# Output products that stream the gated tile, with block transposes as evacuation and one distance between streamed and loaded tiles

## The chip, the cores and the metric

One core of a Trainium2 chip runs the kernel. The metric is the device time of one execution in microseconds, the median of several runs. Shorter is better.

## What is computed

The reference is a gated linear recurrence per head, followed by a feed-forward block:

```python
# q, k, v, a: 4 batches, 8 heads, 768 positions, 48 wide
scale = np.minimum(mag, 0.999) / (mag + 1e-06)     # mag = |a_re + i a_im|
for t in range(S):
    new_re = ar * S_re - ai * S_im
    new_im = ar * S_im + ai * S_re
    kv = np.einsum('bhd,bhe->bhde', k[:, :, t], v[:, :, t])
    S_re, S_im = new_re + kv, new_im
    y[:, :, t] = np.einsum('bhd,bhde->bhe', q[:, :, t], S_re)
...
# x: 3072 tokens x 384; w_gate, w_val: 384 x 1536; w_out: 1536 x 384
g = x @ w_gate
silu = g * (1.0 / (1.0 + np.exp(-g)))
return (silu * (x @ w_val)) @ w_out
```

## The kernel before

**Tiling.** The 3072 tokens are 24 slabs of 128: six chunks of the sequence for each of four batches. Two slabs of one chunk make a group; there are 12 groups, 0 to 11, and groups 10 and 11 hold the last chunk. For each group `stage_ops` loads a, q and k and turns them into scaled queries and keys (ScalarE and VectorE, with cumulative sums over positions on TensorE, lines 500 and 503). For each slab `slab_ops` makes scores (L691, tiles p_ps, "strips" of 64 columns of the array), new states (L757, L760), and then products with the states and with the values (L691 into p_py, strips of 32 columns, four column groups side by side). ScalarE and VectorE copy p_py out as a high part xh and a rest xl (L780, L787), because the matmuls take a reduced 32-bit type (float32r).

**Feed-forward.** `ffn_ops` goes over 12 blocks f of 128 hidden units for each group of 256 tokens. One block is called a step here. f1 (L942) computes gate and value for 128 hidden units x 256 tokens: the weights are the loaded (stationary) tile, xh or xl streams past it, 256 columns; with high and low parts three products for each of three slices of the model width, for gate and value: 18 matmuls. ScalarE applies silu (L948), VectorE multiplies by the value (L953, tile sg), and sg is split again into hh and hl (L354 or L356, L350). f2 (L976) is the output product: hh or hl of 128 tokens is loaded, and 384 columns of the output weights stream; three products for each of two halves of the tokens: 6 matmuls into p_po. In group 0 there are no parts: one product of plain 32-bit floats each. f2 of a block comes one or two f1 later in TensorE's order.

After a group's last f2, `ev` copies each half of p_po to ost, on ScalarE (L354) or on VectorE (L356), and `st` stores ost with one DMA (L990) from SP's queue. p_po is a pair of tiles, one for each half, each with its own bank; the next group's first f2 waits until they are copied out.

**Output weights.** They arrive as doubles in 32-bit words. `c1` to `c3` make plain floats; `c4` casts the high part (lines 354 and 356), `c5` subtracts for the low part (L350). The high and low parts of a block lie behind each other in one tile of 2 x 384 columns.

**Order.** A planner in the program (class `Planner`) fixes the order of all engines' work from costs and due times; each operation is then written out in that order, and each engine works its own list in order. The change leaves the planner's costs and rules alone, so operations stand in the same order after it as before; what an operation issues is different.

**Addresses.** The tiles xh, xl, hh and hl have 128 spare columns; GATED (for hh and hl) and INPUT (for xh and xl) say how many of these come ahead of the data. STILL, with two filler tiles, shifts the weights of f1. These numbers set how far a streamed tile starts from the tile that is loaded. Modulo 512 bytes, worked out from the addresses of the built program, that distance is 192 in every f1, 448 in every f2 of groups 1 to 11, and 128 in the cumulative sums of L503.

```python
TURN_OVER, STILL, GATED, INPUT = 128, 96, 16, 16
...
slots = dict(qs=1, ks=1, T=2, dec=3, sc=2, sg=2, hh=2, hl=2, ost=2, xh=2, xl=2, vt=2, vr=2,
             gv=2, po=1, ps=2, py=1, pm=1)
...
pl.add("oe" + I, {"ACT": 0.4, "DVE": 0.5} if g < NGRP - 1 else {("ACT", "DVE")[i]: 0.45}, ev, deps=[f"f2_{g}.{NF - 1}"], alloc=[("ost", I)], use=[("po", g)], key=key)
```

Of the kernel before, what the change touches and what calls it, by code (L numbers as in the profile page):

```python
# [9 lines left out]
F32 = mybir.dt.float32  # L10
# [4 lines left out]
ALU = mybir.AluOpType  # L15
# [4 lines left out]
P = 128  # L20
# [36 lines left out]

TURN_OVER, STILL, GATED, INPUT = 128, 96, 16, 16
HIGH, LOW, WHOLE = 0, 1, 2
# [171 lines left out]
def quick(ctx, tc, q, k, v, a_re, a_im, w_gate, w_val, w_out, out, count):  # L231
# [3 lines left out]
    const = ctx.enter_context(tc.tile_pool(name="const", bufs=1))  # L235
    still = ctx.enter_context(tc.tile_pool(name="still", bufs=1))
    gap = ctx.enter_context(tc.tile_pool(name="gap", bufs=1))
    work = ctx.enter_context(tc.tile_pool(name="work", bufs=1))
# [20 lines left out]
    turned_v = [const.tile([P, 2, 2, 64], F32, name=f"vr{i}") for i in range(2)]  # L259
    still.tile([P, STILL], F32, name="ahead")  # L260
    gap.tile([P, TURN_OVER - STILL], F32, name="behind")
    W, HALVES = {}, {}
    WIDE = {"w": 2 * DM, "o": DM}

    def place(nm, f, dtype):

        pool = still if nm == "w" else work
        return pool.tile([P, 2 * WIDE[nm]], dtype, name=f"w{nm}{f}", tag=f"w{nm}{f}", bufs=1)
# [52 lines left out]
    def new(tag, inst):  # L321
        if tag in fixed:
            t = fixed[tag][0]
        elif tag[0] in ("ww", "wo"):
            t = None
        elif tag in PSUMS:
            t = psum.tile([P, 512], F32, name="p_" + tag, tag=tag, bufs=2 if tag == "po" else slots[tag])
        else:
            shape, dt = SHAPE[tag]
            if isinstance(inst, tuple) and inst[0] in SPLIT:  # L330
                dt = F32R
            if tag == "xh" and inst == 0:
                dt = F32
            if tag == "xl" and isinstance(inst, str):
                dt = U32
            if tag in ("xh", "xl", "hh", "hl"):
                n = math.prod(shape[1:])
                ahead = GATED if tag in ("hh", "hl") else INPUT
                t = work.tile([P, n + TURN_OVER], dt, name=tag, tag=tag, bufs=slots[tag])[:, ahead:ahead + n]
                if len(shape) > 2:  # L340
                    t = t.rearrange("p (k n) -> p k n", k=shape[1])
            else:
                t = work.tile(shape, dt, name=tag, tag=tag, bufs=slots[tag])
                if tag == "dec":
                    t = t[:, 0:4 * H]
        at_[tag, inst] = t
        return t
# [254 lines left out]
    def slab_ops(n):  # L602
# [80 lines left out]

        def strips(turns, width=32):
# [47 lines left out]
        def states(e):  # L732
# [3 lines left out]
            for slot, kt_, pr, o, heads in blocks():  # L736
                turns[slot] += [(o, gf[:, P * pr + col:P * pr + col + 32], qT(h), kt_ == 0 and i == 0, False)
                                for i, (h, col) in enumerate(heads)]
            strips(turns)

        def values(e):
# [8 lines left out]
            strips(turns)  # L750

# [64 lines left out]
    def weight_ops(f):  # L816
        for nm, n, user in (("w", 2 * DM, "f1"), ("o", DM, "f2")):
# [37 lines left out]
            def c4(e, nm=nm, n=n, whole=whole):  # L855
                W.pop((nm, f - 1, WHOLE), None)
                W[nm, f] = place(nm, f - 1, F32R)
                cast(e, W[nm, f][:, 0:n], whole())

            def c5(e, nm=nm, n=n, whole=whole):  # L860
                tt(e, W[nm, f][:, n:2 * n], whole(), W[nm, f][:, 0:n].bitcast(F32), ALU.subtract)

# [64 lines left out]
    def ffn_ops(g):  # L927
        t0, step = (T1 + (g - 1) * NF * FT, FT) if g else (T0, FT0)
        for f in range(NF):
            I = f"{g}.{f}"  # L930
# [35 lines left out]
            def f2(e, f=f, I=I):  # L966
                hh, hl, h = (at_.get((x, I)) for x in ("hh", "hl", "sg"))
                products = ((hh, HIGH), (hh, LOW), (hl, HIGH)) if g else ((h, WHOLE),)
                if f == 0:
                    new("po", f"{g}.0")  # L970
                    new("po", f"{g}.1")
                for i in range(2):
                    cs = slice(i * P, (i + 1) * P)
                    po = at_["po", f"{g}.{i}"][:, :DM]
                    for j, (l, part) in enumerate(products):
                        nc.tensor.matmul(out=po, lhsT=l[:, cs], rhs=weight("o", f, part),  # L976
                                         start=f == 0 and j == 0, stop=f == NF - 1 and j == len(products) - 1)
            PO = [("po", g)]
# [3 lines left out]
        for i in range(2):  # L982
            b, c = where(2 * g + i)
            I = f"{g}.{i}"

            def ev(e, I=I):
                cast(e, new("ost", I), at_["po", I][:, :DM])

            def st(e, I=I, b=b, c=c):
                nc.sync.dma_start(out=out[b * S + c * P:b * S + (c + 1) * P, :], in_=at_["ost", I])  # L990
            key = t0 + NF * step + 4
# [245 lines left out]
```

## Time and profile before

| | |
|---|---|
| time, median of 3 runs | 629.52 us (629.48 to 631.21) |
| the profiled execution | 629.75 us, of which its span is 628.0 us |
| TensorE matmuls busy | 600.1 us, 96% |
| VectorE busy | 502.0 us, 80% |
| ScalarE busy | 405.2 us, 65% |
| GpSimd busy | 4.2 us, 1% |
| granted clock of TensorE, mean over the span | 0.999 |

PE is TensorE's matmul side, PEld its loading of stationary tiles, DVE VectorE, ACT ScalarE, SPq the queue from which SP issues DMAs. A line such as L942 is a line of the kernel before. In a timeline, matmuls of one form that follow each other share a row (x2); the time behind the start is how long they overlapped in flight, so the pace of TensorE is read from start to start.

### The profile page before, as it was taken

The numbers are of one execution on the slowest core, as the hardware profiler recorded it, in microseconds if no ns is written. First come the engines' busy times: TensorE is split into PE (matmuls) and PEld (weight loads), VectorE is DVE, ScalarE is ACT, GpSimd is POOL, SyncE is SP. The second block draws the span as 40 slices with busy tenths as digits, with TensorE's granted clock in tenths as the row PEclk, the third lists the DMA queues.
The fourth block names the chain that finished last, engine by engine and source line by source line (L and its number), as shares of the span: only waits on it lengthen the run. The fifth ranks groups of instructions, "written<-read, shape, count | busy, mean of one in ns | idle before, by whom it ended". The sixth has DMA issues, their size and how long they took to land.

```text
span 628.0 us, 16113 instructions
## 1 busy us (share of the span) xinstructions
PE 600.1 (96%) x6562; PEld 566.9 (90%) x6562; DVE 502.0 (80%) x931; ACT 405.2 (65%) x653; POOL 4.2 (1%) x15
## 2 busy tenths in 40 slices
PE   2699999989999999999999999999999999999996
PEld 1488788978999899999999999999999999999995
DVE  8999999998997878977989869769879768544432
ACT  7865448886796794857876966976966873212210
POOL 2000000000000000000000000000000000000000
PEclk9999999999999999999999999999999999999999
DMA  8899501233635564455366453554464542331100
GB/s 258 230 301 310 204 27 32 64 124 85 161 106 147 132 149 123 129 139 139 91 148 148 108 153 95 144 156 95 136 166 113 146 121 70 101 103 51 52 1 30
DMA packets 155574, 79.89 MB, mean 127 GB/s; under 512 B 116187, under 2 KB 151261, under 8 KB 155494
## 3 DMA queue, kind: packets, MB, share of 16 engines
q1 hardware_dynamic: 155494, 78.80, 46.1%
q8 instruction: 53, 0.87, 0.6%
q14 instruction: 27, 0.22, 0.1%
HBM read 59.83 MB, written 4.78 MB: 103 GB/s over the span
## 4 chain that ended last, share of the span: by engine, by line
PE 83%; DVE 12%; DMA 1%; issue 1%; ACT 1%; SPq 1%; DVEq 0%
PE p_gv L942 42%; PE p_po L976 21%; PE p_py L691 6%; PE p_ps L691 6%; PE p_pm L503 2%; DVE ww L350 2%; PE p_pm L760 2%; PE p_gv L629 2%; DVE sg L953 1%; DVE s L350 1%; PE p_pm L757 1%; DMA wo<-in_q_dram 1%; DVE ks L350 1%; PE p_gv L500 1%; DVE wo L350 1%
## 5 line engine op out<-in xcount | busy, mean ns | idle before, releaser
L942 PE MATMUL p_gv<-xh,ww 128*128 128x256 f32 x1596 | 303.1, 287 | 2.0 <-DVE sg L953 1.3
L942 PEld LDWEIGHTS p_gv<-xh,ww 128*128 128x128 f32 x1596 | 256.0, 189 | 9.1 <-DVE sg L953 2.7
L942 PE MATMUL p_gv<-xl,ww 128*128 128x256 f32 x726 | 201.2, 277 | 0.0
L1068 ACT ACT_TABLE_LOAD x118 | 151.4, 1283 | 2.1
L942 PEld LDWEIGHTS p_gv<-xl,ww 128*128 128x128 f32 x726 | 136.3, 188 | 0.1
L948 ACT ACTIVATE sg<-p_gv 128x256 f32<-128x256 f32 x144 | 54.9, 384 | 123.7 <-PE p_gv L942 122.3
L976 PE MATMUL p_po<-wo,hh 128*128 128x384 f32 x484 | 125.1, 339 | 0.0
L953 DVE TENSOR_TENSOR sg<-sg,p_gv 128x256 f32<-128x256 f32 x144 | 59.0, 412 | 54.9 <-ACT sg L948 54.6
L976 PEld LDWEIGHTS p_po<-wo,hh 128*128 128x128 f32 x484 | 81.2, 188 | 1.6 <-issue 1.6
L976 PE MATMUL p_po<-wo,hl 128*128 128x384 f32 x242 | 80.7, 334 | 0.0
L350 DVE TENSOR_TENSOR hl<-sg,hh 128x256 fp32r<-128x256 f32 x132 | 54.9, 416 | 7.0 <-ACT hh L354 1.8
L976 PEld LDWEIGHTS p_po<-wo,hl 128*128 128x128 f32 x242 | 45.4, 188 | 0.0
L407 ACT ACTIVATE s<-s 128x768 f32<-128x768 f32 x44 | 36.7, 843 | 9.1 <-DVE s L350 6.7
L691 PEld LDWEIGHTS p_ps<-T 96*64 96x64 f32 x768 | 35.9, 138 | 5.0 <-issue 2.4
L691 PE MATMUL p_ps<-T 96*64 96x128 f32 (+1 forms) x768 | 39.4, 254 | 0.0
L719 DVE TENSOR_TENSOR sc<-p_ps,turn 128x512 f32<-128x512 f32 x48 | 32.1, 685 | 5.0 <-PE p_ps L691 4.8
L780 ACT CAST xh<-p_py 128x384 fp32r<-128x384 f32 x22 | 10.5, 480 | 37.6 <-PE p_py L691 37.5
L356 DVE CAST hh<-sg 128x256 fp32r<-128x256 f32 x87 | 25.2, 290 | 6.1 <-PE p_po L976 2.5
L354 ACT CAST hh<-sg 128x256 fp32r<-128x256 f32 x45 | 18.1, 404 | 18.3 <-DVE sg L953 14.4
L691 PE MATMUL p_py<-sc,vr 128*32 128x128 f32 x384 | 26.0, 273 | 0.9 <-issue 0.9
L691 PE MATMUL p_py<-sc,vt 128*32 128x128 f32 x384 | 25.2, 273 | 0.0
L942 PE MATMUL p_gv<-xh,ww-1_292 128*128 128x256 f32 x132 | 24.8, 280 | 0.0
(142 smaller groups left out, 853.9 us busy)
## 6 DMA issues: line engine op xcount, KB each, us to landing
T<-ww SPq DMA_DIRECT2D x216, 64.0 KB, 2.1
wo<-in_moe_w_out_dram SPq DMA_DIRECT2D x24, 384.0 KB, 4.4
ww<-in_moe_w_gate_dram SPq DMA_DIRECT2D x12, 384.0 KB, 5.8
ww<-in_moe_w_val_dram SPq DMA_DIRECT2D x12, 384.0 KB, 6.6
vt<-in_v_dram SPq DMA_DIRECT2D x24, 192.0 KB, 4.0
out_dram<-ost SPq DMA_DIRECT2D x24, 192.0 KB, 2.3
wo<-in_moe_w_gate_dram SPq DMA_DIRECT2D x12, 384.0 KB, 5.4
wo<-in_moe_w_val_dram SPq DMA_DIRECT2D x12, 384.0 KB, 3.6
```

The lines of the kernel that those rows point to most:

```text
L350: V[e].tensor_tensor(out=out, in0=a, in1=b, op=op)
L354: nc.scalar.copy(out=out, in_=in_)
L356: nc.vector.tensor_copy(out=out, in_=in_)
L407: nc.scalar.activation(out=of(to or dst), in_=of(source), func=func, scale=scale, **kw)
L503: nc.tensor.matmul(out=ps, lhsT=tri, rhs=flat(half(x, i)), start=j == 0, stop=j == 1)
L691: nc.tensor.matmul(out=o, lhsT=l, rhs=r, start=opens, stop=closes, tile_position=(0, width * slot), skip_group_check=True)
L719: nc.vector.tensor_tensor(out=s.rearrange("p (r m) t -> p r m t", m=2), in0=scores[qd].rearrange("p (r m) t -> p r m t", m=2), in1=m, op=A ...
L942: nc.tensor.matmul(out=gv[:, i, :], lhsT=l, rhs=r, start=(m == 0), stop=(m == len(mm) - 1))
L948: nc.scalar.activation(out=new("sg", I), in_=at_["gv", I][:, 0:2 * P], func=AF.Silu)
L953: nc.vector.tensor_tensor(out=sg, in0=sg, in1=at_["gv", I][:, 2 * P:4 * P], op=ALU.mult)
L976: nc.tensor.matmul(out=po, lhsT=l[:, cs], rhs=weight("o", f, part), start=f == 0 and j == 0, stop=f == NF - 1 and j == len(products) - 1)
L1068: nc.scalar.preload_act_table_set(op.load)
```

## The change

- f2 of groups 1 to 10 (`upright` is false): the output weights are loaded, 128 output columns at a time, and hh or hl streams, 256 tokens. For each of three pieces k there are three products: nine matmuls (L982 of the changed kernel) that give the transposed result, output columns by tokens, in one tile p_po of two banks. Groups 0 and 11 keep the six matmuls.
- The output weights' columns are stored in another order (`rows_of`, in `c4` and `c5`), in pieces of 32, so that transposing blocks of 32 x 32 gives rows of the output.
- `ev` of the ten groups is a transpose of 32 x 32 blocks out of p_po, always on VectorE (L998); in the last group it undoes the order of the columns.
- `st` of the ten groups is four DMAs of 32 partitions (L1007), each of pieces of 96 columns.
- GATED and INPUT are 48, and the filler tiles are gone: the distance modulo 512 is 192 in f1 and in the new f2, 320 in f2 of group 11, and 128 still in the cumulative sums.
- In the last chunk, the strips of the products with states and values begin with the fourth column group (`first`).

```diff
-TURN_OVER, STILL, GATED, INPUT = 128, 96, 16, 16
+TURN_OVER, GATED, INPUT = 128, 48, 48
...
-    still.tile([P, STILL], F32, name="ahead")
-    gap.tile([P, TURN_OVER - STILL], F32, name="behind")
...
+    def rows_of(nm, at, plain=False):
+
+        if nm != "o":
+            return at
+        return at.rearrange("p (q k m) -> p q k m", k=KT, q=4) if plain else at.rearrange("p (k q m) -> p q k m", k=KT, q=4)
...
-            t = psum.tile([P, 512], F32, name="p_" + tag, tag=tag, bufs=2 if tag == "po" else slots[tag])
+            t = psum.tile([P, 1024 if tag == "po" else 512], F32, name="p_" + tag, tag=tag, bufs=slots[tag])
...
-                slot = min((s for s in range(len(turns)) if turns[s]), key=lambda s: ends[s])
+                slot = min((s for s in range(len(turns)) if turns[s]), key=lambda s: (ends[s], (s + first) % len(turns)))
...
-            strips(turns)
+            strips(turns, first=1 if c == NCH - 1 else 0)
...
-                cast(e, W[nm, f][:, 0:n], whole())
+                cast(e, rows_of(nm, W[nm, f][:, 0:n]), rows_of(nm, whole(), True))
...
+        upright = g in (0, NGRP - 1)
...
+                wh, wl = (weight("o", f, x).rearrange("p (k n) -> p k n", k=KT) for x in (HIGH, LOW))
+                for k in range(KT):
+                    for j, (l, r) in enumerate(((wh, hh), (wl, hh), (wh, hl))):
+                        nc.tensor.matmul(out=po[:, 2 * P * k:2 * P * k + 2 * P], lhsT=l[:, k, :], rhs=r,
+                                         start=f == 0 and j == 0 and k != 1, stop=f == NF - 1 and j == 2, skip_group_check=True)
...
-                cast(e, new("ost", I), at_["po", I][:, :DM])
+                po, o = at_["po", g], new("ost", I)
...
+                    nc.vector.transpose(out=o.rearrange("p (j k m) -> p k j m", j=4, k=KT),
+                                        in_=po[:, 0:2 * P * KT].rearrange("p (k i j m) -> p k i j m", k=KT, i=2, j=4)[:, :, i])
...
+                for q in range(4):
+                    nc.sync.dma_start(out=r.rearrange("(j a) (q n) -> q a j n", a=32, q=4)[q],
+                                      in_=o[32 * q:32 * q + 32].rearrange("a (j n) -> a j n", j=4))
```

**TensorE, the first f2 of group 1** (p_po is its result; of the two tiles behind the arrow the first streams and the second is loaded; behind them the shape of the result), before:

```order
L503 MATMUL p_pm<-re,tri 128x384
L976 MATMUL p_po<-wo-1_344,hh 128x384 x2
L976 MATMUL p_po<-wo-1_344,hl 128x384
L976 MATMUL p_po<-wo-1_344,hh 128x384 x2
L976 MATMUL p_po<-wo-1_344,hl 128x384
L942 MATMUL p_gv<-xh,ww_880 128x256
L942 MATMUL p_gv<-xl,ww_880 128x256
```

and with the change:

```order
L503 MATMUL p_pm<-re,tri 128x384
L982 MATMUL p_po<-hh,wo-1_336 128x256 x2
L982 MATMUL p_po<-hl,wo-1_336 128x256
L982 MATMUL p_po<-hh,wo-1_336 128x256 x2
L982 MATMUL p_po<-hl,wo-1_336 128x256
L982 MATMUL p_po<-hh,wo-1_336 128x256 x2
L982 MATMUL p_po<-hl,wo-1_336 128x256
L943 MATMUL p_gv<-xh,ww_871 128x256
L943 MATMUL p_gv<-xl,ww_871 128x256
```

The gated tile and the weights have changed places, six matmuls of 384 columns have become nine of 256, and what stands around them is as before.

**VectorE at the end of group 1** (flags are sums that are checked at the end of the program, ks and qs the turned keys and queries of a later group), before:

```order
L350 TENSOR_TENSOR ww_1390<-wo_1387,ww_1390 128x768
L446 TENSOR_REDUCE flags<-re 128x1
L923 TENSOR_REDUCE flags<-ww_1390 128x1
L953 TENSOR_TENSOR sg<-sg,p_gv 128x256
L350 TENSOR_TENSOR ks<-kt,s_1761 128x16x48
```

and with the change:

```order
L350 TENSOR_TENSOR ww_1404<-wo_1401,ww_1404 128x768
L446 TENSOR_REDUCE flags<-re 128x1
L923 TENSOR_REDUCE flags<-ww_1404 128x1
L998 STREAM_TRANSPOSE ost<-p_po 128x3x4x32 x2
L954 TENSOR_TENSOR sg<-sg,p_gv 128x256
L350 TENSOR_TENSOR ks<-kt,s_1784 128x16x48
```

Both evacuations of group 1 come from ScalarE's list into VectorE's, ahead of the product that makes a gated tile. Of the other groups' evacuations four more come over from ScalarE (one each in groups 2, 8, 9 and 10); the rest were on VectorE already.

**SP's queue around the store of a half of group 3** (T is a slab's transposed queries and keys, sent in pieces), before:

```order
L658 DMA T<-ww_1390 32x8x64 x3
L680 DMA vr_89<-in_v_dram 64x2x48 x4
L990 DMA out_dram<-ost 128x384
L658 DMA T<-ww_1390 32x8x64 x9
L990 DMA out_dram<-ost 128x384
```

and with the change:

```order
L658 DMA T<-ww_1404 32x8x64 x3
L680 DMA vr_83<-in_v_dram 64x2x48 x4
L1007 DMA out_dram<-ost 32x4x96 x4
L658 DMA T<-ww_1404 32x8x64 x9
L1007 DMA out_dram<-ost 32x4x96 x4
```

Where one store stood between the pieces of T, four stand now.

## Rows read from the trace of the kernel before

**Rows 1.** page: engines' busy time; the chain that ended last, by engine and line.

```profile
PE 600.1 (96%) x6562; PEld 566.9 (90%) x6562; DVE 502.0 (80%) x931; ACT 405.2 (65%) x653; POOL 4.2 (1%) x15
...
PE 83%; DVE 12%; DMA 1%; issue 1%; ACT 1%; SPq 1%; DVEq 0%
PE p_gv L942 42%; PE p_po L976 21%; PE p_py L691 6%; PE p_ps L691 6%; PE p_pm L503 2%; DVE ww L350 2%; PE p_pm L760 2%; PE p_gv L629 2%; DVE sg L953 1%; DVE s L350 1%; PE p_pm L757 1%; DMA wo<-in_q_dram 1%; DVE ks L350 1%; PE p_gv L500 1%; DVE wo L350 1%
```

**Rows 2.** waits of TensorE: us in total, times, longest.

```profile
PE p_gv L500 <- DMA wo<-in_q_dram: 10.5, 1, 10.5
...
PE p_gv L942 <- DVE sg L953: 1.3, 2, 0.9
```

**Rows 3.** windows: length, then busy us of PE, PEld, DVE, ACT, POOL; clock, DMA.

```profile
100.00:150.00 50.00, 47.09 (x476) 43.65 (x475) 47.66 (x87) 42.22 (x65) 0.00 (x0) 1.00 0.28 79
300.00:400.00 100.00, 100.00 (x1211) 98.03 (x1209) 86.43 (x158) 76.37 (x115) 0.00 (x0) 1.00 0.50 127
```

**Rows 4.** windows: four steps, all lines; one f2, L976 alone.

```profile
347.97:360.38 12.41, 12.41 (x97) 12.38 (x97) 10.29 (x20) 12.23 (x17) 0.00 (x0) 1.00 0.36 87
...
303.68:304.73 1.05, 1.05 (x6) 0.90 (x6) 1.00 0.25 92
```

**Rows 5.** windows, L942 alone (PE, PEld): one f1 behind a cumulative sum, one elsewhere.

```profile
243.43:245.47 2.04, 2.04 (x18) 2.00 (x18) 1.00 1.04 368
232.04:234.16 2.12, 2.12 (x18) 2.08 (x18) 1.00 0.27 76
```

**Rows 6.** windows, L942 alone: five f1 behind value strips; one f1 after the second.

```profile
298.42:300.58 2.16, 2.16 (x18) 2.13 (x18) 1.00 0.00 0
341.57:343.80 2.23, 2.23 (x18) 2.18 (x18) 1.00 0.49 164
386.90:389.07 2.17, 2.17 (x18) 2.13 (x18) 1.00 0.00 0
434.24:436.46 2.22, 2.22 (x18) 2.17 (x18) 1.00 0.00 0
480.89:483.11 2.22, 2.22 (x18) 2.15 (x18) 1.00 0.23 24
...
344.87:346.92 2.05, 2.05 (x18) 2.02 (x18) 1.00 0.77 241
```

**Rows 7.** lines with shapes apart: count | busy us, mean ns of one | idle before.

```profile
L350 DVE TENSOR_TENSOR ks<-kt,s 128x768 f32<-128x768 f32 x22 | 20.9, 950 | 2.3 <-ACT s L407 2.2 <-PE p_pm L760 0.2
...
L649 DVE STREAM_TRANSPOSE ww<-ks 128x768 f32<-128x768 f32 x18 | 17.5, 973 | 1.7 <-DMA T<-ww 1.6
...
L356 DVE COPY ost<-p_po 128x384 f32<-128x384 f32 x16 | 8.6, 548 | 1.7 <-PE p_po L976 1.7
...
L356 DVE CAST wo<-wo 128x384 fp32r<-128x384 f32 x7 | 2.5, 352 | 0.0
```

**Rows 8.** timeline of VectorE and TensorE at the end of group 5.

```profile
357.86 1.01 DVE L356 COPY ost<-p_po 128x384 f32<-128x384 f32 x2
...
359.34 0.34 PE L976 MATMUL p_po<-wo-1_344,hh 128*128 128x384 f32 x1
```

**Rows 9.** end of group 1: window, timeline of ScalarE and of TensorE.

```profile
161.07:172.70 11.63, 11.63 (x90) 11.35 (x88) 11.63 (x18) 10.17 (x18) 0.00 (x0) 1.00 0.57 162
...
163.90 0.85 ACT L354 COPY ost<-p_po 128x384 f32<-128x384 f32 x2
...
173.19 0.39 PE L942 MATMUL p_gv<-xh,ww 128*128 128x256 f32 x1 [0.45 <-DVE sg L953]
```

**Rows 10.** timeline of SP's queue and TensorE near 264 us; page: issues to landing.

```profile
263.51 0.54 SPq L990 DMA_DIRECT2D out_dram<-ost  x1
264.10 5.87 SPq L658 DMA_DIRECT2D T<-ww  x9
...
275.08 0.58 PE L691 MATMUL p_ps<-T 96*64 96x128 f32 x8
...
T<-ww SPq DMA_DIRECT2D x216, 64.0 KB, 2.1
```

More of the change, by code (lines that the diff above doesn't have):

```diff
@@ L265, in place @@
     def place(nm, f, dtype):
-        pool = still if nm == "w" else work
-        return pool.tile([P, 2 * WIDE[nm]], dtype, name=f"w{nm}{f}", tag=f"w{nm}{f}", bufs=1)
+        return work.tile([P, 2 * WIDE[nm]], dtype, name=f"w{nm}{f}", tag=f"w{nm}{f}", bufs=1)
     def spare(nm):
@@ L682, in slab_ops, with strips @@
         pl.add("ldr" + N, {"SP": 2.20}, ldr, deps=[f"ldr{n - 1}"] if n else [], alloc=[("vr", n)], lat=1.4, move=0.8, wary=WARY)
-        def strips(turns, width=32):
+        def strips(turns, width=32, first=0):
             ends = [0] * len(turns)
             while any(turns):
-                slot = min((s for s in range(len(turns)) if turns[s]), key=lambda s: ends[s])
+                slot = min((s for s in range(len(turns)) if turns[s]), key=lambda s: (ends[s], (s + first) % len(turns)))
                 o, l, r, opens, closes = turns[slot].pop(0)
@@ L749, in values @@
                                         c == 0 and kt_ == 0 and i == 0, i == len(heads) - 1))
-            strips(turns)
+            strips(turns, first=1 if c == NCH - 1 else 0)
         def kv(e):
@@ L857, in c4 @@
                 W[nm, f] = place(nm, f - 1, F32R)
-                cast(e, W[nm, f][:, 0:n], whole())
+                cast(e, rows_of(nm, W[nm, f][:, 0:n]), rows_of(nm, whole(), True))
             def c5(e, nm=nm, n=n, whole=whole):
-                tt(e, W[nm, f][:, n:2 * n], whole(), W[nm, f][:, 0:n].bitcast(F32), ALU.subtract)
+                tt(e, rows_of(nm, W[nm, f][:, n:2 * n]), rows_of(nm, whole(), True), rows_of(nm, W[nm, f][:, 0:n].bitcast(F32)), ALU.subtract)
             pl.add("c1" + N, cost(("DVE2",), n), c1, deps=loads + ([f"c3{f - 1}{nm}"] if f else []),
@@ L967, in f2 @@
                 hh, hl, h = (at_.get((x, I)) for x in ("hh", "hl", "sg"))
-                products = ((hh, HIGH), (hh, LOW), (hl, HIGH)) if g else ((h, WHOLE),)
                 if f == 0:
[L970 to L977, printed above, removed]
+                    new("po", g)
+                po = at_["po", g]
+                if upright:
+                    products = ((hh, HIGH), (hh, LOW), (hl, HIGH)) if g else ((h, WHOLE),)
+                    for i in range(2):
+                        for j, (l, part) in enumerate(products):
+                            nc.tensor.matmul(out=po[:, 512 * i:512 * i + DM], lhsT=l[:, P * i:P * i + P], rhs=weight("o", f, part),
+                                             start=f == 0 and j == 0, stop=f == NF - 1 and j == len(products) - 1)
+                    return
+                wh, wl = (weight("o", f, x).rearrange("p (k n) -> p k n", k=KT) for x in (HIGH, LOW))
[3 more added lines that the diff above has]
+                                         start=f == 0 and j == 0 and k != 1, stop=f == NF - 1 and j == 2, skip_group_check=True)
             PO = [("po", g)]
@@ L984, in ffn_ops, with ev @@
             I = f"{g}.{i}"
-            def ev(e, I=I):
-                cast(e, new("ost", I), at_["po", I][:, :DM])
-            def st(e, I=I, b=b, c=c):
-                nc.sync.dma_start(out=out[b * S + c * P:b * S + (c + 1) * P, :], in_=at_["ost", I])
+            def ev(e, i=i, I=I):
+                po, o = at_["po", g], new("ost", I)
+                if upright:
+                    part = po[:, 512 * i:512 * i + DM]
+                    cast(e, *((rows_of("o", x, plain) for x, plain in ((o, True), (part, False))) if g else (o, part)))
+                else:
+                    nc.vector.transpose(out=o.rearrange("p (j k m) -> p k j m", j=4, k=KT),
+                                        in_=po[:, 0:2 * P * KT].rearrange("p (k i j m) -> p k i j m", k=KT, i=2, j=4)[:, :, i])
+            def st(e, I=I, b=b, c=c):
+                r, o = out[b * S + c * P:b * S + (c + 1) * P, :], at_["ost", I]
+                if upright:
+                    nc.sync.dma_start(out=r, in_=o)
+                    return
+                for q in range(4):
+                    nc.sync.dma_start(out=r.rearrange("(j a) (q n) -> q a j n", a=32, q=4)[q],
+                                      in_=o[32 * q:32 * q + 32].rearrange("a (j n) -> a j n", j=4))
             key = t0 + NF * step + 4
```

2 lines of the change are left out of this document (removed).

## The prediction

> **What bounds the kernel now.** I read the page first: TensorE is busy for 600.1 of 628.0 us and carries 83% of the chain that ended last, the gate and value products (L942, from here f1) 42% and the output products (L976, f2) 21% [rows 1]. The view of waits says where TensorE is not the bound: its long wait is the first load, and later only short waits on VectorE are left [rows 2]. By stage, from 300 to 400 us TensorE is busy throughout and VectorE for 86 of 100 us; from 100 to 150 us VectorE is the fuller one, 47.66 to 47.09 of 50 [rows 3]. So from group 2 on the time is the sum of TensorE's steps, and I price the change by the start times of its matmuls. Their busy time is no price: it contains overlap.
>
> A step is one f1 (18 matmuls of 256 columns) and one f2 (6 of 384). Four steps in a row take 12.41 us, 3.1025 each (96 matmuls; one more touches the edge); one f2 takes 1.05 us [rows 4] and one f1 2.05 [rows 6]. That is 0.114 us for 256 columns and 0.175 for 384: the wide form costs more per column, not less.
>
> The second thing to see is that f1 has two beats. Behind cumulative sums 18 matmuls take 2.04 us, 0.1133 each; at other places the same 18, same shapes, take 2.12 us, 0.1178 each [rows 5]. Both keep their beat through the whole f1. Of the five f1 that directly follow value strips (those of the second slab, groups 5 to 9), two are on the short beat (2.16 and 2.17 us, the first gap included) and three on the long one (2.22 to 2.23) [rows 6]. After the first of the long ones, one f2 suffices and the next f1 is back at 2.05 [rows 6].
>
> **The change, part by part.**
>
> 1. Output products. Nine matmuls of 256 columns replace six of 384: as many columns (2304). They now have f1's shape, and, by the constants, f1's distance between the streamed and the loaded tile. So I give them f1's price. On the short beat a step becomes 27 x 0.1133 = 3.06 us. Against 3.1025 that is a gain of 0.0425. Groups 2 to 10 have 108 such steps in the stretch where TensorE is the bound: 108 x 0.0425 = 4.6 us gained. Group 1's twelve would give 0.5 more, but lie where VectorE is as full as TensorE; I count them as nothing and keep 0.5 as the lower end. The last group keeps six wide products, at another distance (320 instead of 448 bytes): as much as -0.5 (12 x 0.0425) or +1.0 (12 x 18 x 0.0045, its f1 on the long beat); I take 0.
>
> 2. What removes the gain. Before, f2 had another distance than f1, and the long beat died at the next f2. Now nothing between two slabs has another distance except the cumulative sums. A long step costs 27 x (2.12 - 2.04) / 18 = 0.12 us more. In the new order of TensorE 67 steps' worth of matmuls lie between strips and the next cumulative sum, most of it in nine stretches behind the second slab of a group, of mostly seven steps. Bounds: none of them long (0), or all 67 (+8.0). The three long f1 of [rows 6] stand at the head of stretches that now have 7.0, 7.7 and 6.7 steps, 21.4 in all, +2.6. The strips take over a rhythm from what is ahead of them, which the change makes more uniform, so I take two such stretches, 14 steps: +1.7. This is my choice, the least certain term.
>
> 3. Evacuation. Ten groups turn their blocks on VectorE, two transposes each; six of these twenty evacuations were ScalarE's. A 768-column transpose takes 973 ns where a 768-column product takes 950, and a 384-column copy out of PSUM 548 [rows 7]; I price a 384-column transpose as that copy, 0.55 (bounds 0.49, half of 973, and 0.97). In rows that follow each other a copy occupies 0.47 to 0.5 of VectorE's line (two in 1.01) [rows 8]. Where they stay on VectorE, nothing is added. Both transposes now need the whole of the group's last f2, and the next group's first f2 needs both; the tightest place is 357.86 us, where both copies are done at 358.87 and the f2 starts at 359.34 [rows 8]: 0.47 us of cover, which 0.55 each does not use up (at 0.97 each they would end 0.46 late; +2 at most if four groups are so). The place that hurts is group 1. There ScalarE did both, at 163.90, while VectorE had no idle time from 161.07 to 172.70, and TensorE then waits for VectorE's gated tile at 173.19 [rows 9]. Two transposes in that line move everything by 2 x 0.47 = 0.95 us, and TensorE with it: +0.95 (bounds 0 and 1.1). The other four moved ones meet VectorE idle time or a late stage: 0.
>
> 4. Weights and last evacuation. The casts and differences of the output weights now run in pieces of 32 columns. A cast on VectorE takes 352 ns; at the plain rate it would be 548 [rows 7], seven of them, +1.4 at most. Products that write runs of 48 out of 96 columns cost the 950 ns of any other [rows 7], so I take 0. The same holds for the two last copies.
>
> 5. Stores. SP issues four stores instead of one, 60 more in all. In the tightest place one store (0.54 us) stands in front of nine pieces of a slab's transposed tile, the last issued at about 269.4, and the strips that need it start at 275.08 [rows 10]. Pieces take 5.87 / 9 = 0.65 each to issue, so three more stores delay them by 1.6 to 2.0 us; 5.7 are there, of which 2.1 go to landing [rows 10]. Cover holds: 0. If it were used up twice, +1.
>
> 6. Strips of the last chunk start with the fourth column group: the same 128 matmuls of states and values, rotated. Price 0; what it can do is set the beat after it, which is term 2.
>
> Sum: -4.6 + 1.7 + 0.95 = -1.95 us on the profiled execution of 629.75 us (span 628.0, 1.75 around it), which lies 0.23 above the median. Against the median of 629.52: **627.6 us**.
>
> **Rivals.**
>
> *The long beat stays* (slower). From 30 long steps on ((4.6 - 0.95) / 0.12) the gain is gone. For it: three of five in [rows 6], and f2 no longer ends it. Against: behind cumulative sums the f1 of [rows 5] is on the short beat, so they may end it. With 22 to 45 long steps 628.5 to 631.3; with all 67, 629.5 - 3.65 + 8.0 = 633.9.
>
> *A price per matmul* (slower). Nine matmuls instead of six could cost three times some fixed amount, with the weights of f2 now loaded as 128-column pieces of another tile. Then f2 goes at f1's highest row, 9 x 0.1178 = 1.06 against 1.05, at least no gain, +1.1 for 108 steps, and with 0.95 and 0 to 1 for f1: 631.6 to 632.6. Against: 0.114 per 256 and 0.175 per 384 columns leave no positive fixed part.
> The Trainium skill (TensorE: Matmul & The Clock Gate, Back-to-back issue gap) has such a fixed part: it gives columns / 2.4 + 2.5 ns for an isolated matmul at full clock. By that, an estimate from its formula, nine of 256 take 0.983 us and six of 384 0.975, so the change would lose 0.8 us over 108 steps instead of gaining 4.6. The trace disagrees on the wide one: 0.175 us against the formula's 0.1625 [rows 4].
>
> *TensorE is not let go faster.* VectorE at 86% [rows 3], or SP's 60 issues, sets the pace: the gain of term 1 stays out, 629.5 to 630.5. Against: the waits of [rows 2].
>
> **How the numbers follow.** Forecast (0 to 21 long steps, 625.9 to 628.5, centre 627.6): 0.52. Long beat, 22 to 45 steps: 0.22, and above: 0.13. Price per matmul: 0.05. Not let go: 0.08. About 0.3%, 1.9 us, can be told from no change, so faster means below 627.6 and slower above 631.4. Faster: most of the forecast's lower part, 0.46 with the reach of its bounds; same: its rest, most of the first long-beat case and the last rival, 0.33; slower: 0.21. Range: from the forecast with no long step and group 1's 0.5 and a part of its free evacuation, 624.8, to 45 long steps with a late piece, 631.8.
>
> **What would show it.** Right: nine starts of f2 in 1.02 to 1.03 us, f1 behind it at 2.04; transposes of about 0.55 us; TensorE waiting about 1 us more near 166 to 175 us; in most groups no 2.12. Wrong: f1 at 2.12 over whole stretches behind strips (the long beat), or f2 at 1.05 and more (a price per matmul), or new waits of TensorE after 200 us.

## The result and the profile after

The changed kernel takes **638.0 us** (median of 8 runs, 633.6 to 643.6) against 629.96 for the kernel before in the same session: 1.0123 times as long, 95% interval 1.0092 to 1.0154 (the ratio is of the fast runs and leaves out the longest). Forecast were 627.6 us, with a range up to 631.8: the wrong side, and outside the range.

The profiled execution took 639.87 us, its span is 638.2. Ten microseconds of it, at 17 to 27 us, ran at half clock in the start-up part. What that cost can't be read off: in profiles without such a stretch the first f1 of group 2 starts from 1.6 us before the kernel before's (experiment 5) to 0.9 us behind it (experiment 3). So only differences between two places of one column of the table below are read, not its first row. The page of the changed kernel, busy times and chain, beside [rows 1]:

```profile
PE 603.3 (95%) x6922; PEld 569.7 (89%) x6922; DVE 504.1 (79%) x937; ACT 402.2 (63%) x647; POOL 4.2 (1%) x15
...
PE 78%; DVE 9%; ACT 4%; DMA 4%; SPq 2%; issue 1%; DVEq 0%
```

TensorE's share of the chain fell from 83 to 78%; ScalarE, DMA and SP's queue now hold 10% together, against 3% before. Its waits, beside [rows 2]:

```profile
PE p_gv L943 <- DVE sg L954: 5.7, 4, 2.5
...
PE p_po L976 <- DVE sg L954: 2.6, 2, 2.1
...
PE p_po L982 <- DVE ost L998: 0.6, 1, 0.6
```

The wait for the gated tile grew from 1.3 to 5.7 us. Where the time came from is read from the start of the same f1 in both traces, each counted from its span's start (differences to before in us; the columns on the right are experiments that follow):

```
start of f1            before   after   one    group 1   four stores,  addresses,
                                        store  as before before        before
group 2, first         156.74   +0.29   -1.30   +0.86     -0.08         +0.32
group 2, seventh       176.39   +2.21   -0.39   +0.85     -0.07         +0.33
group 5, first         301.63   +2.98   -1.57   +0.20     +1.03         +0.80
group 5, eighth        328.36   +7.93   -1.79   +3.37     +3.95         +1.34
group 10, first        537.45   +8.70   -1.58   +3.96     +4.71         +4.04
group 11, seventh      600.61   +9.64   -0.65   +4.89     +4.71         +5.25
```

Two steps stand out: 1.92 us at the end of group 1, and 4.95 in the middle of group 5. The rest of the path from +0.29 to +9.64, 2.5 us, is small pieces.

**The stop in group 5.** Timeline of SP's queue, then of VectorE, then of TensorE, in the changed kernel:

```profile
314.02 1.96 SPq L1007 DMA_DIRECT2D out_dram<-ost  x4
316.02 5.89 SPq L658 DMA_DIRECT2D T<-ww  x9
322.01 3.25 SPq L1007 DMA_DIRECT2D out_dram<-ost  x4
...
321.78 0.56 DVE L356 CAST s<-im 128x768 fp32r<-128x768 f32 x1
325.36 0.98 DVE L649 STREAM_TRANSPOSE ww<-ks 128x768 f32<-128x768 f32 x1 [3.02 <-DMA out_dram<-ost]
326.26 0.38 DVE L954 TENSOR_TENSOR sg<-sg,p_gv 128x256 f32<-128x256 f32 x1
...
326.70 0.39 PE L943 MATMUL p_gv<-xh,ww 128*128 128x256 f32 x1 [2.50 <-DVE sg L954]
```

The same place in the kernel before, timeline of SP's queue and of VectorE:

```profile
310.92 0.54 SPq L990 DMA_DIRECT2D out_dram<-ost  x1
311.50 5.87 SPq L658 DMA_DIRECT2D T<-ww  x9
...
318.51 0.56 DVE L356 CAST s<-im 128x768 fp32r<-128x768 f32 x1
318.98 0.97 DVE L649 STREAM_TRANSPOSE ww<-ks 128x768 f32<-128x768 f32 x1
```

Read it from the top. The four stores take 1.96 us of SP's queue where one took 0.54, and nine pieces of T stand behind them. T is read out of the buffer ww, and there is one such buffer: the next slab's transposes on VectorE overwrite it, so they must wait until the last piece has been read. Before, that piece landed at 318.79 (from the trace's semaphore events) and VectorE came to the transpose at 318.98: 0.19 us of room at the most, and perhaps none, since the transpose that waits here began 0.39 us after the landing. After, it landed at 324.97, and VectorE stood still for 3.02 us. Behind the transpose in VectorE's list is the gated tile sg, and TensorE waits for that. The profile puts VectorE's wait down to the store, its guess by the last event; the experiment on before below tells that it is T.

About half of this wait does not seem to be the stores' issue time. In the traces a transfer lands in sixteen parts, each with a semaphore event. Fifteen parts of the last piece of T had landed at 323.41; the sixteenth came 1.56 us later. From 322.52 on, for 1.42 us, a packet of 16384 bytes of the queue that the profile calls instruction (q8) was under way. DMA queues of the changed kernel from 311 to 331 us (packets, MB, share of 16 engines):

```profile
q8 instruction: 1, 0.02, 0.4%
```

In this trace 45 of the 216 pieces of T have a last part more than 0.7 us behind the one before it. Such a packet was under way during 40 of these 45, and during 32 of the other 171. That it holds the part up is read from this coincidence and was not tested. Without the late part the wait would be about 1.5 us, an estimate (323.41 and 0.39, less 322.34, where VectorE's list had got to). The profiles of experiments 1, 4 and 5 have the late part and the packet at this place too; experiment 9 has the stop without them.

What follows the wait makes it dearer. Windows of the changed kernel: stretches of the stop with all lines (clock in the third column from the end), then the f1 that follows, L943 alone:

```profile
320.00:327.70 7.70, 5.20 (x43) 4.88 (x42) 4.51 (x8) 4.19 (x7) 0.00 (x0) 1.00 0.43 103
327.70:331.10 3.40, 3.40 (x18) 3.40 (x18) 1.10 (x4) 1.65 (x4) 0.00 (x0) 0.50 1.07 240
...
326.70:330.14 3.44, 3.44 (x18) 3.15 (x18) 0.64 0.90 230
```

TensorE stood for 2.5 us, and a microsecond after it began again the granted clock was at its lower level, 1.2 GHz (0.50), for 3.4 us. The f1 took 3.44 us instead of 2.04 to 2.12.

**The end of group 1.** Timelines of VectorE and TensorE, beside [rows 9]:

```profile
165.16 1.03 DVE L998 STREAM_TRANSPOSE ost<-p_po 128x384 f32<-128x384 f32 x2
...
174.38 0.55 DVE L894 TENSOR_REDUCE flags<-wo 128x1 f32<-128x384 f32 x1 [0.82 <-DMA wo<-in_moe_w_gate_dram]
...
175.32 0.39 PE L943 MATMUL p_gv<-xh,ww 128*128 128x256 f32 x1 [1.48 <-DVE sg L954]
```

The two transposes stand in VectorE's full line for 0.96 us (to the next start at 166.12). Then VectorE waits 0.82 us more for a load of weights, another transfer of SP's queue. Together they are 1.78 of the step's 1.92. The last part of this load came late too: the fifteenth landed at 173.09, the sixteenth at 174.36, with a packet of the instruction queue under way from 170.58 to 172.44.

**The beats.** Windows, one line at a time, beside [rows 4] and [rows 5]: four steps with all lines, two f1 and two new f2, and a wide f2 of the last group with the f1 behind it:

```profile
262.78:275.02 12.24, 12.24 (x110) 12.24 (x109) 11.36 (x24) 12.09 (x16) 0.00 (x0) 1.00 0.45 102
...
262.78:264.82 2.04, 2.04 (x18) 2.01 (x18) 1.00 0.75 204
304.61:306.73 2.12, 2.12 (x18) 2.07 (x18) 1.00 0.26 49
...
264.82:265.84 1.02, 1.02 (x9) 0.99 (x9) 1.00 0.22 38
303.55:304.61 1.06, 1.06 (x9) 1.01 (x9) 1.00 0.00 0
...
602.86:603.91 1.05, 1.05 (x6) 0.89 (x6) 1.00 0.47 112
603.91:606.03 2.12, 2.12 (x18) 2.08 (x18) 1.00 0.11 26
```

On the short beat four steps take 12.24 us, 3.06 each, as forecast. But by the start times of all 132 f1 with parts, 51 are on the long beat (10 before), and 45 of the 120 new f2. The beat holds through f1 and f2 alike, in stretches of up to some 13 steps behind value strips, and in the last group, with its distance of 320, all twelve f1 are long.

### The profile page after: what moved, and what is told of

Its sections match the earlier page's. It is cut to its first block, busy times and chain, and to the rows that moved or that the text cites. A ratio compares the mean times of both kernels' runs of the same rounds, so it can differ in the third digit from the quotient of the medians.

```text
span 638.2 us, 16898 instructions
## 1 busy us (share of the span) xinstructions
PE 603.3 (95%) x6922; PEld 569.7 (89%) x6922; DVE 504.1 (79%) x937; ACT 402.2 (63%) x647; POOL 4.2 (1%) x15
## 4 chain that ended last, share of the span: by engine, by line
PE 78%; DVE 9%; ACT 4%; DMA 4%; SPq 2%; issue 1%; DVEq 0%
PE p_gv L943 42%; PE p_po L982 16%; PE p_py L691 5%; PE p_ps L691 5%; PE p_po L976 4%; PE p_pm L503 2%; PE p_pm L760 2%; PE p_gv L629 1%; ACT L1086 1%; SPq L658 1%; SPq L1007 1%; DVE ww L350 1%; ACT s L407 1%; DMA vr<-in_v_dram 1%; DMA ww<-in_a_im_dram 1%
## 5 line engine op out<-in xcount | busy, mean ns | idle before, releaser
L943 PE MATMUL p_gv<-xh,ww 128*128 128x256 f32 x1596 | 306.2, 289 | 6.3 <-DVE sg L954 5.7
L943 PEld LDWEIGHTS p_gv<-xh,ww 128*128 128x128 f32 x1596 | 257.5, 190 | 13.6 <-DVE sg L954 7.0
L943 PE MATMUL p_gv<-xl,ww 128*128 128x256 f32 x726 | 202.4, 279 | 0.0
L943 PEld LDWEIGHTS p_gv<-xl,ww 128*128 128x128 f32 x726 | 137.0, 189 | 0.2 <-issue 0.2
L982 PE MATMUL p_po<-hh,wo 128*128 128x256 f32 x660 | 120.6, 280 | 0.0
L982 PEld LDWEIGHTS p_po<-hh,wo 128*128 128x128 f32 x660 | 101.5, 189 | 1.6 <-issue 1.6
L982 PE MATMUL p_po<-hl,wo 128*128 128x256 f32 x330 | 92.0, 279 | 0.0
L982 PEld LDWEIGHTS p_po<-hl,wo 128*128 128x128 f32 x330 | 62.4, 189 | 0.0
L894 DVE TENSOR_REDUCE flags<-wo 128x1 f32<-128x384 f32 x36 | 19.6, 543 | 14.3 <-DMA wo<-in_moe_w_gate_dram 7.0
L899 ACT ACTIVATE wo<-wo 128x384 f32<-128x384 f32 x36 | 20.0, 555 | 10.8 <-DMA wo<-in_moe_w_gate_dram 7.3
```

The lines of the kernel that those rows point to most:

```text
L899: nc.scalar.activation(out=high(0), in_=high(1), func=AF.Square, accum_out=flags[:, fl_hi + j:fl_hi + j + 1])
L943: nc.tensor.matmul(out=gv[:, i, :], lhsT=l, rhs=r, start=(m == 0), stop=(m == len(mm) - 1))
L982: nc.tensor.matmul(out=po[:, 2 * P * k:2 * P * k + 2 * P], lhsT=l[:, k, :], rhs=r, start=f == 0 and j == 0 and k != 1, stop=f == NF - 1 an ...
```

## The experiments

Ratios are to the kernel before, in the same session on the same chip, with 95% intervals.

**1. Another distance for the new f2.** `GATED = 112`: 448 modulo 512 instead of 192, the wide f2 of the last group at 64.

```diff
-TURN_OVER, GATED, INPUT = 128, 48, 48
+TURN_OVER, GATED, INPUT = 128, 112, 48
```

> The changed kernel with GATED at 112 instead of 48: the streamed hh and hl of the new f2 lie 448 bytes (modulo 512) from the loaded weights, as in the old f2, while f1 stays at 192. Theory A (the long beat lives on because f1 and f2 have one distance): no long f1 after the first of a stretch, at most 15 f1 of 132 at 2.12 us instead of the 51 of the changed kernel's profile, and 3 to 5 us less time, about 633 to 635, if nine products at 448 cost no more than 1.03 us. Theory B (SP's 60 extra stores hold back the pieces of T and with them everything) and theory C (the moved evacuation): no difference, about 638.

636.24 us, 1.0100 (1.0067 to 1.0132). The long beat stays: 36 f1 and 31 f2. Windows of L982 in this run, two f2:

```profile
283.09:284.15 1.06, 1.06 (x9) 1.02 (x9) 1.00 0.32 63
304.62:305.64 1.02, 1.02 (x9) 0.98 (x9) 1.00 0.29 90
```

So nine products at 448 take over either beat; it isn't enough for f2 to have another distance than f1. The stop in group 5 is there (4.2 us). Theory A fails by its own figures: at most 15 long f1 and 633 to 635 us were expected.

**2. One store for each half.**

```diff
-                for q in range(4):
-                    nc.sync.dma_start(out=r.rearrange("(j a) (q n) -> q a j n", a=32, q=4)[q],
-                                      in_=o[32 * q:32 * q + 32].rearrange("a (j n) -> a j n", j=4))
+                nc.sync.dma_start(out=r, in_=o)
```

> The changed kernel with one store for each half of a group instead of four; it writes the same bytes in rows of 384 columns as the kernel before did, so the output's columns stand in wrong places. Theory B: the wait of 3.0 us of VectorE's transposes for pieces of T near 322 us and the 2.5 us wait of TensorE behind it are gone, 3 to 5 us less, 633 to 635. Theory A and C: at most 1 us less, 637 to 638, and runs still spread over several us.

**630.53 us**, 1.0018 (1.0003 to 1.0032): of 8.0 us, 1.2 are left. Timelines of SP and VectorE at the place of the stop:

```profile
308.93 0.54 SPq L1003 DMA_DIRECT2D out_dram<-ost  x1
309.51 5.87 SPq L658 DMA_DIRECT2D T<-ww  x9
...
317.28 0.97 DVE L649 STREAM_TRANSPOSE ww<-ks 128x768 f32<-128x768 f32 x1
```

No wait at the transpose, and in the table above no step in group 5. Group 1 costs 0.91 us here: the second wait there, for the load of weights, is gone too. The load is issued behind the stores, at 169.45 with four and at 165.06 with one. But the wait has other causes as well, since with four stores from SP it is 0.82, 1.03, 0.28 and 0.03 us (changed kernel, experiments 1, 4 and 5). The long beat is rarer, but stays (40 f1, 31 f2).

**3. Group 1 with six wide products and both copies as before.**

```diff
-        upright = g in (0, NGRP - 1)
+        upright = g in (0, 1, NGRP - 1)
```

> The changed kernel with group 1 done as before: six products of 384 columns and evacuation by ScalarE in its place, so that no transpose stands in VectorE's line near 164 us. Theory C: between the first f1 of group 2 and its sixth, 1.9 us are lost in the changed kernel against the kernel before (157 to 175 us); here 0 to 0.4, and the time falls by 1 to 2 us, to about 636 to 637. Theories A and B: no difference beyond the spread of the beats.

635.37 us, 1.0100 (1.0066 to 1.0133). In the table the step at group 1's end is gone (0.86 to 0.85), the stop in group 5 is not (0.20 to 3.37).

**4. Strips of the last chunk not rotated.** `first=0` in both calls of `strips`.

> The changed kernel without the rotation of the last chunk's strips (they begin with the first column group as in the kernel before). If the rotation sets the beat behind those strips, the stretches behind slabs 20, 22 and 23 change from long and short beats (changed kernel: long behind 20, short behind 22, long behind 23) to others, worth up to 12 x 0.12 = 1.5 us either way: 636.5 to 639.5. If the rotation does nothing, the same beats and 638.

636.28 us, 1.0132 (1.0076 to 1.0188), as with the change. Its profile has fewer long beats (36 f1, 27 f2), but the times don't tell that apart. No effect that can be separated.

**5. Four stores of whole rows.** The same number of DMAs, but each of 32 whole rows, 1536 bytes a piece instead of 384.

```diff
-                    nc.sync.dma_start(out=r.rearrange("(j a) (q n) -> q a j n", a=32, q=4)[q],
-                                      in_=o[32 * q:32 * q + 32].rearrange("a (j n) -> a j n", j=4))
+                    nc.sync.dma_start(out=r[32 * q:32 * q + 32], in_=o[32 * q:32 * q + 32])
```

> The changed kernel with four stores for each half as before, but each of 32 whole rows of 384 columns (1536-byte pieces instead of 384-byte pieces; the output's columns stand in wrong places). Theory B1 (what costs is the time SP takes to issue three more stores ahead of the pieces of T): the stop in group 5 stays, 4 us between its sixth and eighth f1, and the time stays at 635 to 638. Theory B2 (the small pieces hold up the DMA engines): the time is that of one store, about 630.5.

635.01 us, 1.0091 (1.0068 to 1.0114), with the stop in group 5 (3.1 us between its sixth and eighth f1, where 4 were expected). It is the number of the DMAs, not the size of their pieces.

**6. The four stores from GpSimd's queue.** `nc.gpsimd.dma_start` instead of `nc.sync.dma_start`.

> The changed kernel with its four stores of 384-byte pieces, all outputs right, issued from GpSimd's queue instead of SP's. Theory B1: as with one store, 630 to 631.5, no stop in group 5. Theory B2: the pieces are the same, the stop stays, 635 to 638. If issuing from GpSimd holds VectorE up, something in between, with longer VectorE instructions around the stores.

633.78 us, 1.0061 (1.0038 to 1.0084). No step in group 5 (-0.32 before, -0.34 after the place). Smaller stops have come in elsewhere, the largest 1.59 us, at 458. Timeline of VectorE there:

```profile
454.07 0.96 DVE L472 SCALAR_TENSOR_TENSOR s<-s,s 128x768 f32<-128x768 f32 x1 [1.46 <-ACT s L407]
456.59 0.98 DVE L649 STREAM_TRANSPOSE ww<-ks 128x768 f32<-128x768 f32 x1 [1.56 <-DMA s<-fr]
```

VectorE waits at the same transposes again, at another slab, with no store ahead of the pieces of T on SP. The last piece's fifteenth part landed at 454.63 and its sixteenth at 456.20, 0.39 us before the transpose; a packet of 16384 bytes of the instruction queue was under way from 453.59 to 454.53. So this stop has the mark of the late part alone.

**7. One store, and nine products at 64.** Experiment 2 with `GATED = 16`: the wide f2 of the last group is at 448 again, as before.

> One store (columns in wrong places) and GATED 16: the nine products lie at a distance of 64, the last group's wide f2 at 448 as in the kernel before. If the wide f2 of 384 columns at 448 ends the long beat, and the nine products keep it whatever their distance (as at 448 in the first experiment): the last group's twelve f1 go at 2.04 to 2.06 instead of 2.12, 0.8 us less than with one store alone, 629.7; the long stretches ahead of it stay. If distance does not matter at all: 630.5 and the last group at 2.12.

634.75 us, 1.0086 (1.0062 to 1.0109): worse than experiment 2, a miss. Windows of L943 and L982, an f1 and the f2 behind it:

```profile
345.48:347.52 2.04, 2.04 (x18) 2.01 (x18) 1.00 0.77 233
...
347.52:348.58 1.06, 1.06 (x9) 1.02 (x9) 1.00 0.59 219
```

At 64 every one of the 120 new f2 is long, even behind a short f1. Of the last group's twelve f1, eleven stayed long, though its wide f2 are at 448, where they were expected short.

**8. Stores from GpSimd, groups 1 and 10 wide, `GATED = 16`.** Experiments 3, 6 and 7 put together.

> All outputs right: stores from GpSimd's queue, groups 1 and 10 with six wide products and plain evacuation, GATED 16 (wide f2 at 448). If the three causes add up: no stop in group 5 (that is 630.5), no shift behind group 1 (0.9 less), no long beat in groups 10 and 11 (12 steps of group 10 at 3.10 instead of a mix of 3.06 and 3.18, 0.8 less in group 11): 628.3 to 629.3, at or just under the kernel before (629.4). If GpSimd's issuing costs VectorE, 630 or more.

634.4 us, 1.0074 (1.0056 to 1.0093), where 628.3 to 629.3 were expected: no gain. All nine-product f2 are long again, and of the 24 f1 of groups 10 and 11, with wide f2 at 448 between them, 21 are long, where none were expected.

**9. The kernel before with four stores.** The other way round: only the stores are split, by 32 whole rows.

```diff
-                nc.sync.dma_start(out=out[b * S + c * P:b * S + (c + 1) * P, :], in_=at_["ost", I])
+                for q in range(4 if 0 < g < NGRP - 1 else 1):
+                    r = slice(32 * q, 32 * q + 32) if 0 < g < NGRP - 1 else slice(0, P)
+                    nc.sync.dma_start(out=out[b * S + c * P:b * S + (c + 1) * P, :][r], in_=at_["ost", I][r])
```

> The kernel before, unchanged but for the stores of groups 1 to 10: each half goes out in four DMAs of 32 partitions (32 whole rows) from SP instead of one. Theory (SP's issue time of the four stores, ahead of the pieces of T, holds up the next slab's transposes on VectorE and so TensorE near 320 to 336 us): the same stop in group 5 as with the change, 3 to 5 us later at 346 us than before, TensorE's wait for the gated tile of 3 us or more, and 633 to 635 us. Rival (the stop needs the change's other parts too: the transposes as evacuation, or TensorE's faster products ahead of it): within 1 us of before, 629 to 631 us, and no wait over 1 us there.

632.99 us, 1.0065 (1.0044 to 1.0085). The stop comes at the same place. Timelines of SP, VectorE and TensorE:

```profile
312.54 1.93 SPq L992 DMA_DIRECT2D out_dram<-ost  x4
314.51 5.88 SPq L658 DMA_DIRECT2D T<-ww  x9
320.49 1.94 SPq L992 DMA_DIRECT2D out_dram<-ost  x4
...
322.24 0.98 DVE L649 STREAM_TRANSPOSE ww<-ks 128x768 f32<-128x768 f32 x1 [2.09 <-DMA out_dram<-ost]
...
323.58 0.40 PE L942 MATMUL p_gv<-xh,ww 128*128 128x256 f32 x1 [1.82 <-DVE sg L953]
```

Neither the transposes nor the new f2 are needed for it. The last piece of T landed at 321.85 and the transpose began 0.39 us later, as far behind as in the changed kernel (324.97 and 325.36); the first of the stores behind it landed at 322.25, after the transpose had begun, so it cannot be what VectorE waited for. TensorE's wait is shorter here (1.82, where 3 or more were expected), no half clock follows, and the step in group 5 is 2.9 us against 4.95 in the changed kernel. The last piece's sixteenth part is not late here (0.04 us behind the fifteenth, 1.56 in the changed kernel): this is the price of the stores' issue alone. A smaller stop of the same kind stands in group 4, where the transpose at 274.21 waits 1.82 us; in that group the path grows from +0.02 to +1.04.

**10. The kernel before with the new addresses.** GATED and INPUT 48, no filler tiles: f1 at 192, every wide f2 at 320.

```diff
-TURN_OVER, STILL, GATED, INPUT = 128, 96, 16, 16
+TURN_OVER, GATED, INPUT = 128, 48, 48
```

> The kernel before with only the new addresses: GATED and INPUT 48, no filler tiles, so the distance between streamed and loaded tile is 192 in f1 and 320 in the six wide products of every group, 12 of them as in the last group of the changed kernel. Theory D (a wide f2 at 320 doesn't end the long beat, one at 448 does): f1 on the long beat in 40 to 130 of 132, wide f2 still 1.05, no stop in group 5; each long f1 costs 0.08 us, so 632 to 639 us. Rival (the last group's twelve long f1 have to do with what stood ahead of it, not with 320): as before, about 10 long f1, 629 to 631 us.

636.66 us, 1.0115 (1.0086 to 1.0144). No stop; the path grows evenly. 106 of 132 f1 are on the long beat. Windows of L937 (f1 of this kernel) and L971 (f2):

```profile
346.20:348.31 2.11, 2.11 (x18) 2.07 (x18) 1.00 0.81 204
...
348.31:349.36 1.05, 1.05 (x6) 0.89 (x6) 1.00 0.71 266
```

So in the kernel before the addresses alone make the long beat frequent: with the old form of f2 the new ones cost 7.3 us (636.66 less 629.36), and theory D's figures came. That it is f2's distance, 320 against 448, is not shown: in experiments 7 and 8 f1 is at 192 and the wide f2 at 448, as in the kernel before, and the long beat goes on. Without the filler tiles the weights of f1 stand elsewhere, and xh and xl with INPUT; which of these does it was not tried.

**11. One store, and group 1 as before.** Experiments 2 and 3 together.

> The changed kernel with one store for each half (the columns of nine groups' results land in the wrong order) and with six wide products in group 1 as well as in groups 0 and 11. If the parts add up: the changed kernel's loss of group 1's evacuation (0.9 to 1.9 us in the profiles) goes on top of what one store gives back, so 0.3 to 1.9 us under the run with one store alone: 628.6 to 630.2 us, that is between 0.8 us under and 0.8 us over before. If it is over 630.5 us, group 1's evacuation wasn't what stood between one store and before, and the long beat alone takes the gain of the nine products.

631.97 us, 1.0046 (1.0026 to 1.0066), 628.2 to 634.0 in ten runs: over 630.5, the point from which group 1's evacuation was not to be what stands between one store and before. In the times undoing group 1 gains nothing (631.97 against 630.53 with one store alone, in another session). The profile is of the fastest of these runs, and there the step at group 1's end is gone (-1.01 to -1.02). What the slower runs did differently no trace shows; the beat is a candidate, since its stretches differ from profile to profile, but that wasn't tested.

**12. The four stores from ScalarE's queue, group 1 as before.**

> The changed kernel with the four stores of each half issued from ScalarE's queue instead of SP's, and with six wide products in group 1. Theory (what hurts is the issue time on SP ahead of the pieces of T): no stop in group 5; if a store costs ScalarE little, 629 to 631 us. Rival: ScalarE, which now waits for VectorE's transposes ahead of its stores, comes late with the gated tile's sigmoid and with the high part hh behind it, and TensorE waits for them at the end of each group: 632 us or more, with new waits of TensorE for ScalarE or VectorE at several group ends.

651.3 us, 1.0362 (1.0338 to 1.0386): the rival. Timelines of ScalarE's queue and of TensorE in group 3:

```profile
208.93 5.19 ACTq L1007 DMA_DIRECT2D out_dram<-ost  x6
214.16 0.84 ACT L407 ACTIVATE s<-s 128x768 f32<-128x768 f32 x1 [6.13 <-DMA out_dram<-ost]
...
216.38 0.58 PE L943 MATMUL p_gv<-xh,ww 128*128 128x256 f32 x1 [4.50 <-DVE sg L954]
```

ScalarE stands for its stores as SP does, and the work behind them, the silu of the next gated tile among it, comes late.

None of these beats the kernel before. A second buffer for the transposes, which would take the wait away and leave the stores, was not tried: it needs 6 KB of each partition. Nor was an order of SP's queue with the stores behind the pieces of T.

## Why the prediction was wrong

**Term 5, "Cover holds: 0", is the step that failed, and the largest.** It counted the SP time of the stores nearly right (three more, 1.6 to 2.0 us; measured 1.42, that is 1.96 for four less 0.54 for one), but looked at one reader of T only, the strips, which had 5.7 us. The other user is the buffer that T comes out of. There the room in group 5 was 0.19 us, so a delay goes through. The sign stood in [rows 7]: the transposes ww<-ks had 1.7 us of idle time before them, 1.6 of it behind T<-ww. One of these waits lies at the very place that was read for the strips [rows 10], behind the pieces of T issued from 264.10. VectorE in the kernel before:

```profile
272.90 0.98 DVE L649 STREAM_TRANSPOSE ww<-ks 128x768 f32<-128x768 f32 x1 [0.53 <-DMA T<-ww]
```

The last part of this transfer came late too (272.78, the fifteenth at 271.38), and was all of this wait; but with four stores the wait is 1.70 us in the changed kernel and 1.82 in experiment 9, where no part was late. The row was used for the price of a transpose and not for its wait. The bound of +1 was therefore no bound. By experiment 2 the three more stores cost 6.9 us (8.0 less 1.2), by experiment 9 3.6 without the rest of the change. What adds to the 3.6 in the changed kernel is shown in part: the late part of T's last piece, TensorE's half clock behind the longer wait, and the wait at group 1's end; their shares were not taken apart.

The Trainium skill says of DMAs (DMA: Bandwidth & Descriptors, Issuing engines are not separate DMA queues) that issuing from several engines saves only the time to initiate them, usually small beside the DMA itself. One store's 0.49 us of issue (1.96 / 4) is small beside the stores' 2.1 us to landing in the changed kernel, as the page says; nine pieces behind four such stores are where that time decided. The Trainium skill's rule to use one transfer of 128 partitions rather than two to halves of them (DMA: Bandwidth & Descriptors, Rules for kernel authors) speaks against this part of the change, and the runs agree that one is better (630.53 against 638.0); the reason that they show is the issue time, where the page says that the two serialize.

**Term 2, the long beat, was mis-sized.** Taken were 14 long steps, the bound 67. Measured were 40 long f1 and 31 long f2 with one store, 51 and 45 in the changed kernel's profile. Thirty more long f1 than before at 0.08 us and 31 long f2 at 0.04 are 3.6 us, an estimate from these counts, against 1.7 for term 2 and 0 for the last group, which has twelve of the f1. The two stretches were chosen because the strips were to take over a rhythm from what is ahead of them; no run shows that they do. It assumed that the cumulative sums, at a distance of 128, end the long beat; experiment 1 has long f1 on both sides of one (the f2 at 283.09 stands ahead of a sum, and the f1 behind it goes on at 0.118 a matmul). Without the stores' stop the rival "the long beat stays", 628.5 to 631.3 us for 22 to 45 long steps, is what happened: 630.53. That it lands in that band is in part luck, as the last group's long f1 are in it and were not in the rival.

**Term 1** was right in price: 1.02 us for nine products, 3.06 for a step. It holds on the short beat alone, so less than the 4.6 us came. The last group, taken as 0 with a bound of +1.0, went towards the bound: twelve long f1, which in experiment 2 cost 0.43 us over the first six (-1.08 at its first f1, -0.65 at the seventh). The rival of a price per matmul falls: on the short beat nine products take 1.02 us, and where they take 1.06 at 192, the f1 beside them are long too.

**Term 3** was right in the profiles: 0.95 forecast, 0.91 in experiment 2 and nothing with group 1 wide; the times of experiment 11 don't show it. The transposes took what was assumed. Tile ost in the changed kernel:

```profile
L998 DVE STREAM_TRANSPOSE ost<-p_po x20: 536/572/584, 165.2 to 598.3; 128x384 f32<-128x384 f32 x20
```

0.57 us against 0.55. At the group ends TensorE waits for one only 0.6 us, once. **Terms 4 and 6**: for 6 experiment 4 shows nothing that could be told apart; 4 was not tried alone.

## What to carry to other kernels

Where a DMA is split, price the added issue time against every piece behind it in the queue, and for each of these ask twice: who reads what it writes, and who wants to overwrite what it reads. A row that says an instruction already waits for a transfer says that its cover there is zero. And put the cheap half of a change into the kernel before by itself: the stores alone there, one edit (experiment 9), show 3.6 us where the prediction had 0. Where a wait behind a DMA differs between profiles, look whether the last of its sixteen parts came late beside a packet of the instruction queue.

## What the runs showed of the hardware

- The same 18 matmuls of 256 columns keep one of two beats, 0.1133 or 0.1178 us each at full clock, through f1, f2 and at times cumulative sums, mostly until strips come. The nine products join either beat at distances of 192 and 448 modulo 512 and are always long at 64; with the new addresses the long beat goes on through wide f2 at 320 (106 of 132 f1, experiment 10) and at 448 (21 of 24, experiment 8), with the old ones at 448 it is rare (10 of 132). What in the chip makes the beat is not shown.
- The length of a wait of TensorE does not say whether the clock falls. Waits of 2.50 us (changed kernel), 2.38 (experiment 1) and 2.30 (experiment 4) in group 5 were followed by 3.4 us at the lower level, one of 2.42 at the same place (experiment 5) was not, nor were 1.82 (experiment 9) and 2.49 (experiment 12, at 421.79).
- Pieces of T usually land about 2.1 us after their issue; one part in sixteen of some comes 0.7 us or more behind the others, mostly with a 16384-byte packet of the instruction queue under way (40 of 45 in the changed kernel, 34 of 35 in the kernel before).
- A store's issue has a median of 430 ns on SP and of 551 ns on GpSimd's queue (changed kernel and experiment 6, 80 stores each):

```profile
L1007 SPq DMA_DIRECT2D out_dram<-ost x80: 315/430/1714, 165.8 to 603.2; - x80
...
L1007 POOL DMA_DIRECT2D out_dram<-ost x80: 548/551/911, 165.5 to 595.9; - x80
```
